# A second MLP computed in two phases through DRAM, its first product by a seven-product scheme

## The chip, the cores and the metric

One Trainium2 chip; the kernel runs on one of its cores. The metric is the device time of one execution in microseconds. Three executions of the kernel before took 925.81, 926.36 and 927.38 us, median 926.36.

## What is computed

Attention over 4 sequences of 576 tokens with 8 heads of 64, a window of 128 and a linear bias by distance; its output, 2304 tokens of 512, goes through two MLPs one after the other. The change is about the second.

```python
x = attention(q, k, v)                       # 2304 x 512
h = x @ w_in1                                # 2304 x 2048
g = where(h > 0, h, exp(min(h, 0)) - 1)
x = g @ w_out1                               # 2304 x 512
h = x @ w_in2                                # 2304 x 2048
g = maximum(0.01 * h, h)
return g @ w_out2                            # 2304 x 512
```

The weights arrive in float64. Everything is returned in float32.

## The kernel before

**Numbers.** Each float32 operand of an MLP product is split into a high part of type float32r (a cast on ACT) and a low part (a subtraction on DVE), and a product is the sum of three: high x high, high x low, low x high (split_mm). A weight in float64 is read as pairs of 32-bit words and turned into float32 by w_a1 and w_a2 on ACT and w_ts and w_add on DVE; w_hi and w_lo then split it.

**Tiles.** d_ff is cut into 16 pieces c of 128 (NC), d_model into 4 slices of 128 (NK), the tokens into blocks (BLK1 for the first MLP, BLK2 for the second), four of 512 and one of 256. For a block and a piece, the first product (mlp1_h, mlp2_h) has weights as the stationary operand and tokens as the moving one: 4 slices x 3 terms = 12 matmuls into one PSUM bank. ACT and DVE make g from it, split into high and low. The second product accumulates over the 16 pieces. In mlp1_y, w_out is stationary and tokens move; its output, still feature by token, is written to the DRAM tensor x2T. In mlp2_y, g's tokens are stationary (128 at a time) and 512 columns of w_out move; its banks hold rows of the output.

**Order.** All matmuls keep the order of the program (keep_in_program_order). Instructions on ACT, DVE, POOL and SP are ordered ahead of time by a planner with estimated durations, priority being the program's order; some runs of them (Ordered) are kept as written. Each engine then issues in that fixed order. Attention is interleaved with the first MLP's blocks. The last block of the first MLP (J = 4, lines 762 to 774) is interleaved with the second MLP's first block of 256 tokens, and layer 2's weights are converted there and later by w_tick. Then the second MLP runs block by block, mlp2_h one or two pieces ahead of mlp2_y (todo2, pend2).

**Buffers.** A tag names a ring of buffers. "w0" to "w15" hold one converted piece of weights each, or other things before and after; "eg", "gh" and "gl" hold g and its two parts, three buffers each; the eight PSUM banks are "y0" to "y3", "s0", "s1", "h" and "c".

Lines of the profile: L122 is the matmul in the helper matmul, and L113 the call in Ordered; so PE is read by tile names. h_ps is the first product of either MLP (layer 2's are written at line 699), y the second of layer 1, o_y, o_s and o_c the second of layer 2. L172 and L177 are w_a1 and w_a2, L533 to L537 the ELU and split in mlp1_h, L566 and L568 the evacuation of y, L684 to L688 the load and split of x2, L701 to L706 the leaky ReLU and split in mlp2_h.

Of the kernel before, what the change touches and what calls it, by code (L numbers as in the profile page):

```python
# [10 lines left out]
F32 = mybir.dt.float32  # L11
# [17 lines left out]
NB = NT // BLK  # L29

BLK1 = [(0, 512), (512, 256), (768, 512), (1280, 512), (1792, 512)]
BLK2 = [(0, 256), (256, 512), (768, 512), (1280, 512), (1792, 512)]


STAGING = [4 + c for c in range(12)] + [13, 14, 15, "pool"] + ["extra", "pool"] * 8
STAGED = (3, 2)
W1_EARLY = 12
LOADS = "ppppwppwppwwppwwwwwwww"

# [7 lines left out]
QK = 2 * BLK + P  # L47
FIRST_STARTS = [5, 9, 13, 15]
Y_LAG = 2
LAG2 = 4  # L50


def slope(h):
# [31 lines left out]
def attention_elu_leaky_kernel(  # L85
# [55 lines left out]


    W, raws, mids = {}, {}, {}
    pieces = [(layer, c) for layer in (1, 2) for c in range(NC)]
    at = {"load": 0, "a": 0, "b": 0, "c": 0}

    def w_load():
        k = at["load"]
        at["load"] += 1
        layer, c = pieces[k]  # L150
        w_in, w_out = ((w_in1, w_out1), (w_in2, w_out2))[layer - 1]

        kind = STAGING[k]
        if kind == "pool":
            raw = wrawp.tile([P, 2, DM, 2], I32, tag="wraw", name="wraw")
        elif kind == "extra":
            raw = extra.tile([P, 2, DM, 2], I32, tag="wraw2", name="wraw")
        else:
            raw = wp.tile([P, 2, DM, 2], I32, tag=f"w{kind}", name="wraw")
        for io, src in enumerate((w_in[c], w_out[c * P:(c + 1) * P, :])):  # L160
# [3 lines left out]
    def w_a1(k):  # L164
        high = raws[k][:, :, :, 1]
        f = wfp.tile([P, 2, DM], I32, tag="wf", name="wf")
# [57 lines left out]

    def w_tick(last):

        while at["load"] < min(last, max(at["c"] + STAGED[at["load"] >= NC], W1_EARLY)):
# [273 lines left out]
    def mlp1_h(J, cs, late_work=lambda: None):  # L501
# [3 lines left out]

        n = BLK1[J][1]
        xh, xl = X1[J]

        last = J == len(BLK1) - 1
# [28 lines left out]
        return hi, lo  # L538

    Y = {}  # L540
    xrp = None

    def mlp1_y(J, cs, gg):
        gh, gl = gg
# [9 lines left out]
                             start=cs[ci] == 0 and i == 0 and m % per == 0, stop=cs[ci] == NC - 1 and i == 2,  # L554
                             skip_group_check=True)
        if cs[-1] == NC - 1:
            if J == len(BLK1) - 1:

                all_ys = xrp.tile([P, NK, n], F32, tag="xr", name="xr")
            for i, y in enumerate(Y.pop(J)):  # L560
                if J == len(BLK1) - 1:
# [111 lines left out]
    attn.close()  # L673


    xrp = ctx.enter_context(tc.tile_pool(name="xr", bufs=1))
    gl2 = ctx.enter_context(tc.tile_pool(name="gl2", bufs=2))
    extra = ctx.enter_context(tc.tile_pool(name="wraw2", bufs=1))
    X2, O = {}, {}

    def x2_load(i):
        t0, n = BLK2[i]
        xr = xrp.tile([P, NK, n], F32, tag="xr", name="xr")
        nc.sync.dma_start(out=xr, in_=x2T[:, :, t0:t0 + n])  # L684
        x2 = x1p.tile([P, 2, NK, n], F32R, tag="x1", name="x2")
        for m in range(NK):
            nc.scalar.copy(x2[:, 0, m, :], xr[:, m, :])
            nc.vector.tensor_tensor(x2[:, 1, m, :], xr[:, m, :], x2[:, 0, m, :].bitcast(F32), op=ALU.subtract)  # L688
        X2[i] = x2[:, 0], x2[:, 1]

    def mlp2_h(i, c, k):
        n = BLK2[i][1]
        xh, xl = X2[i]
        ps = psp.tile([P, n], F32, tag="s0" if k < NC - LAG2 else ("h", "s0", "s1", "c")[k % (4 if i > 1 else 2)],
                      name="h2_ps")
        wih, wil = weights(2, c, 0)
        for kk in range(NK):
            s = slice(kk * P, (kk + 1) * P)
            split_mm(ps, wih[:, s], wil[:, s], xh[:, kk, :], xl[:, kk, :], kk == 0, kk == NK - 1)
        g = egp.tile([P, n], F32, tag="eg", name="g2")  # L700
        nc.scalar.activation(g, ps, AF.Prelu, alpha=0.01)  # L701
        pool = gl2 if k % 2 else glp
        hi = pool.tile([P, n], F32R, tag="gh", name="g2h")
        lo = pool.tile([P, n], F32R, tag="gl", name="g2l")
        nc.scalar.copy(hi, g)  # L705
        nc.vector.tensor_tensor(lo, g, hi.bitcast(F32), op=ALU.subtract)  # L706
        return hi, lo

    def mlp2_y(i, c, gg):
        t0, n = BLK2[i]  # L710
        hi, lo = gg
        woh, wol = weights(2, c, 1)
        if c == 0:
            O[i] = [psp.tile([P, DM], F32, tag=tg, name=f"o_{tg}")
                    for tg in (("y0", "y1", "y2", "y3") if i else ("s1", "c"))]
        for s in range(n // P):
            r = slice(s * P, (s + 1) * P)
            split_mm(O[i][s], hi[:, r], lo[:, r], woh, wol, c == 0, c == NC - 1)
            if c == NC - 1:
                rows = slice(t0 + s * P, t0 + (s + 1) * P)  # L720
                if i < len(BLK2) - 1:
                    os_ = egp.tile([P, DM], F32, tag="eg", name="os")
                else:

                    if s == 0:
                        O["os"] = xrp.tile([P, NK, DM], F32, tag="xr", name="xr")
                    os_ = O["os"][:, s]
                if i == len(BLK2) - 1 and s == n // P - 1:

# [12 lines left out]

    todo2 = [(0, c) for c in range(NC - LAG2)]
    for c in range(LAG2):
        todo2 += [(1, c), (0, NC - LAG2 + c)]
    todo2 += [(i, c) for i in range(1, len(BLK2)) for c in range(NC) if i > 1 or c >= LAG2]
    pend2, k = [], 0  # L750

    def mlp2():
        nonlocal k
        i, c = todo2[k]
        pend2.append((i, c, mlp2_h(i, c, k)))
        k += 1
        if i and c == 6 and i + 1 < len(BLK2):
            x2_load(i + 1)
        if len(pend2) > (1 if k <= NC - LAG2 else 2):
            mlp2_y(*pend2.pop(0))  # L760

    x2_load(0)
    J = len(BLK1) - 1
    for c in range(NC):
        g = mlp1_h(J, [c])
        mlp1_y(*pend.pop(0))
        pend.append((J, [c], g))
        while at["c"] < NC + c - Y_LAG:
            w_tick(2 * NC)
        if c >= LAG2:  # L770
            mlp2()
    x2_load(1)
    for x in pend:
        mlp1_y(*x)
# [57 lines left out]
```

## Time and profile before

| | us |
|---|---|
| median of three runs | 926.36 |
| the profiled execution | 926.94 |
| its span | 925.20 |
| PE busy | 914.6 |
| DVE busy | 407.1 |
| ACT busy | 403.8 |
| POOL busy | 118.0 |

PE is the matmul engine, DVE the vector engine, ACT the scalar engine, POOL the general one; SP only issues DMAs. The span is cut into stretches: the start and attention alone (to 63 us), attention with the first MLP (to 433 us), the first MLP's last block (433 to 566 us, with layer 2's first block beside it), the rest of the second MLP (to 919 us) and the tail. Busy times are sums over instructions; for PE they include waits that the pipeline hides, so its idle time is read from stretches and waits, and the price of one matmul in a stream from the chain of work, which counts only the time by which the end moves on.

### The profile page before, as it was taken

The page shows a single profiled execution, that of the slowest core. Times are in us where ns is not written, and L with a number is a line of the kernel's source. Part 1 is how long each engine was busy: PE and PEld are TensorE (multiplying, and loading weights), DVE is VectorE, ACT ScalarE, POOL GpSimd, SP SyncE. Part 2 cuts the span into 40 slices and gives each one's busy share as a digit, 9 for nine tenths or more (in the row PEclk, how much of TensorE's full clock was granted, in tenths as well). Part 3 has the DMA queues.
Part 4 walks back from the last instruction along what each step waited for, and adds up shares of the span by engine and source line. Part 5 has one row for each costly group of instructions (what it writes and reads, how often), then busy time and mean ns, then how long its engine had stood idle before and what let it go on. Part 6 is the DMA issues. An engine that isn't in the chain of part 4 may idle for free.

```text
span 925.2 us, 13025 instructions
## 1 busy us (share of the span) xinstructions
PE 914.6 (99%) x4885; PEld 747.9 (81%) x4885; DVE 407.1 (44%) x1034; ACT 403.8 (44%) x918; POOL 118.0 (13%) x281
## 2 busy tenths in 40 slices
PE   8999999999999999999999999999999999999998
PEld 5578878998887787888788888888888888888886
DVE  6798865655444454453566675211311131112111
ACT  7897854444344344333566665322322232222222
POOL 5702222323222211220000000000000000000000
PEclk9999999999999999999999999999999999999999
DMA  9842322222111021001244334100200010001001
GB/s 335 324 160 64 111 91 92 69 69 70 33 37 45 22 89 46 24 10 69 91 182 137 137 137 137 46 23 1 91 1 1 0 46 1 1 1 45 1 1 46
DMA packets 38495, 66.77 MB, mean 72 GB/s; under 512 B 3488, under 2 KB 22944, under 8 KB 38432
## 3 DMA queue, kind: packets, MB, share of 16 engines
q1 hardware_dynamic: 37712, 64.76, 20.4%
q10 hardware_dynamic: 720, 1.18, 0.3%
q8 instruction: 38, 0.62, 0.3%
q14 instruction: 25, 0.20, 0.1%
HBM read 56.49 MB, written 9.44 MB: 71 GB/s over the span
## 4 chain that ended last, share of the span: by engine, by line
PE 91%; DMA 6%; ACT 1%; DVE 1%; issue 0%; SPq 0%; ACTq 0%; DVEq 0%
PE h_ps L122 41%; PE y L122 20%; PE o_y L122 19%; PE s_ps L122 4%; PE av_ps L122 3%; DMA wraw<-in_w_out 3%; PE pt_ps L419 2%; DMA qkvr<-in_qkv 1%; PE o_s L122 1%; PE o_c L122 1%; DMA vr<-in_vp 1%; ACT wraw L177 0%; ACT wf L172 0%; DVE eg L535 0%; DMA x2T<-ys 0%
## 5 line engine op out<-in xcount | busy, mean ns | idle before, releaser
L122 PE MATMUL h_ps<-x,w 128*128 128x512 f32 (+1 forms) x1920 | 425.2, 370 | 1.7 <-DVE eg L535 0.7
L122 PEld LDWEIGHTS h_ps<-x,w 128*128 128x128 f32 x1920 | 335.4, 188 | 71.3 <-ACT x L113 4.0
L706 DVE TENSOR_TENSOR g2l<-g,g2h 128x512 fp32r<-128x512 f32 (+1 forms) x80 | 51.0, 637 | 272.3 <-ACT g2h L705 272.3
L122 PE MATMUL y<-gh,w 128*128 128x512 f32 (+1 forms) x640 | 157.7, 368 | 0.5 <-DVE ys L566 0.5
L122 PE MATMUL o_y<-w,g2h 128*128 128x512 f32 x512 | 157.7, 389 | 0.0
L701 ACT ACTIVATE g<-h_ps 128x512 f32<-128x512 f32 (+1 forms) x80 | 44.3, 554 | 255.3 <-PE h_ps L122 255.3
L122 PEld LDWEIGHTS y<-gh,w 128*128 128x128 f32 x640 | 113.8, 189 | 20.9 <-DVE ys L566 0.9
L122 PEld LDWEIGHTS o_y<-w,g2h 128*128 128x128 f32 x512 | 96.1, 188 | 20.0
L122 PE MATMUL o_y<-w,g2l 128*128 128x512 f32 x256 | 99.6, 389 | 0.0
L113 POOL TENSOR_SCALAR t<-t,stat 128x128 f32<-128x128 f32 (+3 forms) x160 | 71.5, 460 | 90.8 <-DVE stat L113 85.8
L113 ACT ACTIVATE t<-t,stat 128x128 f32<-128x128 f32 (+2 forms) x160 | 62.5, 393 | 42.6 <-DVE t L113 29.5
L533 ACT ACTIVATE eg<-h_ps 128x512 f32<-128x512 f32 (+1 forms) x80 | 44.0, 550 | 80.8 <-PE h_ps L122 78.6
L122 PE MATMUL y<-gl,w 128*128 128x512 f32 (+1 forms) x320 | 78.7, 368 | 0.0
L536 ACT CAST gh<-eg 128x512 fp32r<-128x512 f32 (+1 forms) x80 | 46.2, 577 | 73.9 <-DVE eg L535 67.0
L113 POOL TENSOR_SCALAR_AFFINE_SELECT pt<-pt 128x256 f32<-128x256 f32 (+1 forms) x112 | 45.2, 412 | 213.3 <-ACT pt L431 209.8
L537 DVE TENSOR_TENSOR gl<-eg,gh 128x512 fp32r<-128x512 f32 (+1 forms) x80 | 51.2, 640 | 38.3 <-ACT gh L536 38.1
L122 PEld LDWEIGHTS y<-gl,w 128*128 128x128 f32 x320 | 56.9, 189 | 10.0
L534 DVE TENSOR_SCALAR eg<-eg 128x512 f32<-128x512 f32 (+1 forms) x80 | 32.3, 405 | 63.1 <-ACT eg L533 61.2
L122 PEld LDWEIGHTS o_y<-w,g2l 128*128 128x128 f32 x256 | 48.1, 188 | 9.9
L113 DVE CUSTOM_DVE_ANT_0 t<-s_ps,bias 128x256 f32<-128x256 f32 (+4 forms) x160 | 51.6, 370 | 3.8 <-PE s_ps L122 3.2
L535 DVE TENSOR_TENSOR eg<-h_ps,eg 128x512 f32<-128x512 f32 (+1 forms) x80 | 50.9, 637 | 2.5
L705 ACT CAST g2h<-g 128x512 fp32r<-128x512 f32 (+1 forms) x80 | 46.2, 578 | 2.3
(60 smaller groups left out, 677.7 us busy)
## 6 DMA issues: line engine op xcount, KB each, us to landing
wraw<-in_w_in SPq DMA_DIRECT2D x32, 512.0 KB, 4.2
wraw<-in_w_out SPq DMA_DIRECT2D x32, 512.0 KB, 5.4
qkr<-in_kT SPq DMA_DIRECT2D x28, 192.0 KB, 2.8
xr<-x2T SPq DMA_DIRECT2D x4, 1024.0 KB, 5.3
qkr<-in_qT SPq DMA_DIRECT2D x28, 128.0 KB, 2.6
out<-os SPq DMA_DIRECT2D x14, 256.0 KB, 2.0
vr<-in_vp SPq DMA_DIRECT2D x16, 192.0 KB, 2.5
x2T<-ys SPq DMA_DIRECT2D x12, 256.0 KB, 2.6
```

The source lines that it names most:

```text
L113: ins = f(*args, **kw)
L122: tc.keep_in_program_order(nc.tensor.matmul(*args, **kw))
L419: tc.keep_in_program_order(nc.tensor.transpose(ps[:nk, col:col + n], t[:n, c:c + nk], ident[:n, :n]))
L533: nc.scalar.activation(g[:, :m], ps, AF.Exp)
L534: nc.vector.tensor_scalar(g[:, :m], g[:, :m], 1.0, -1.0, op0=ALU.min, op1=ALU.add)
L535: nc.vector.tensor_tensor(g[:, :m], ps, g[:, :m], op=ALU.max)
L536: nc.scalar.copy(hi[:, :m], g[:, :m])
L537: nc.vector.tensor_tensor(lo[:, :m], g[:, :m], hi[:, :m].bitcast(F32), op=ALU.subtract)
L701: nc.scalar.activation(g, ps, AF.Prelu, alpha=0.01)
L705: nc.scalar.copy(hi, g)
L706: nc.vector.tensor_tensor(lo, g, hi.bitcast(F32), op=ALU.subtract)
```

## The change

The second MLP is done in two phases. Phase one computes g for all tokens and writes it to a DRAM tensor g2T; phase two reads it back and does the second product.

In phase one, tokens are taken in 3 groups of 768 and d_ff in 8 pairs of pieces, 24 units. In a unit the first product is a 2 x 2 block product: two halves of the group (384 tokens), two halves of d_model (2 slices each), two pieces of d_ff. Strassen's scheme in Winograd's form makes the four blocks of the result from 7 block products. The sums of tokens (t1 to t4) are made by DVE (x2_job), the sums of weights by POOL (in_convert), the sums of results by DVE and by accumulating products in one bank. Products 1 and 2 share bank x, 6, 7 and 4 bank y, 5 and 3 bank z; two units' banks alternate. On PE the order is unit_a of a unit, unit_c of the unit before, unit_b.

Weights w_in2 are converted during the last block of layer 1, w_out2 in units 17 to 23 and in phase two's first block. That block of layer 1 has no matmuls of layer 2 beside it any more. In phase two, g2T is loaded four pieces at a time, split (g2_split), and used by mlp2_y as before. The block of 256 tokens is now the fourth of five.

The diff, cut:

```diff
+GRP = 768
+HALF = GRP // 2
+NP2 = NC // 2
+NU = NG * NP2
+OPERANDS = ("b11", "t2", "t1", "b21", "t3", "t4", "b22")
+OP_OF = {1: "b11", 2: "b21", 3: "b22", 4: "t4", 5: "t1", 6: "t2", 7: "t3"}
+W_OF = {1: 3, 2: 4, 3: 7, 4: 6, 5: 0, 6: 1, 7: 2}
...
-        tag = "s0" if last and cs[0] < LAG2 and (LAG2 - cs[0]) % 2 else "h"
-        if not last and cs[0] % 2 != (J == 0):
-            tag = "c"
+        tag = "c" if cs[0] % 2 != (J == 0) else "h"
...
-                if J == len(BLK1) - 1:
-                    ys = all_ys[:, i * per:i * per + per]
+                if i == 3:
+                    ys = glp.tile([P, per, n], F32, tag="gh", name="ys")
...
+    def in_convert(p):
+        k = ("in", p)
+        s = wp.tile([P, 8, 2 * P], F32, tag=f"w{p}", name="s")
+        w_ts(k)
...
+        dve.tensor_tensor(four.bitcast(I32), mids.pop(k), raw[:, :, :, 0], op=ALU.add)
+        for o, x, y, op in ((0, 5, 6, ALU.add), (1, 0, 3, ALU.subtract), (2, 3, 5, ALU.subtract), (7, 4, 1, ALU.subtract)):
+            pool.tensor_tensor(s[:, o], s[:, x], s[:, y], op=op)
...
+    def split_w(u, part):
+        s = S[u % NP2]
+        if part == 2:
+            t = wfp.tile([P, 2, 2, 2 * P], F32R, tag="wf", name="h2")
+            hi, lo = t[:, 0], t[:, 1]
+            cuts = [(0, 2, 6)]
+            H2[u] = hi, lo
+        else:
+            hi = wp.tile([P, 5, 2 * P], F32R, tag=f"w{8 + u % 2 * 2}", name="h1")
+            lo = wp.tile([P, 5, 2 * P], F32R, tag=f"w{9 + u % 2 * 2}", name="l1")
+            cuts = [(3, 5, 0), (0, 3, 0)]
+            H1[u] = hi, lo
+        for a, b, o in cuts:
+            nc.scalar.copy(hi[:, a:b], s[:, a + o:b + o])
+            nc.vector.tensor_tensor(lo[:, a:b], s[:, a + o:b + o], hi[:, a:b].bitcast(F32), op=ALU.subtract)
...
+    def x2_job(g, n):
...
+        def sub(o, x, y):
+            nc.vector.tensor_tensor(o, x, y, op=ALU.subtract)
+        def split(name, src):
...
+            nc.scalar.copy(t[:, 0], src)
+            nc.vector.tensor_tensor(t[:, 1], src, t[:, 0].bitcast(F32), op=ALU.subtract)
...
+        if n == 0:
+            split("b11", b(0, 0))
+            sub(b(0, 0), b(0, 1), b(0, 0))
+            sub(b(0, 1), b(1, 1), b(0, 1))
+        elif n == 1:
+            split("t1", b(0, 0))
+            sub(b(0, 0), b(1, 1), b(0, 0))
...
+    def product(m, u, bank, start):
...
+        for kk in range(2):
+            s = slice(kk * P, (kk + 1) * P)
+            split_mm(bank, wh[:, s], wl[:, s], xh[:, kk, :], xl[:, kk, :], start and kk == 0, kk == 1,
+                     skip_group_check=True)
...
+    def unit_a(u):
...
+        product(1, u, x, True)
+        s1 = small(glp, "gh", "s1")
+        nc.scalar.copy(s1, x)
+        product(6, u, y, True)
+        a = small(glp, "gl", "a")
+        nc.vector.tensor_tensor(a, y, s1, op=ALU.add)
+        product(5, u, z, True)
...
+    def unit_b(u):
+        product(2, u, x, False)
+        c11 = small(glp, "gh", "c11")
+        g2_out(u, 0, 0, c11, x)
+        product(7, u, y, False)
+        b = small(glp, "gl", "b")
+        nc.vector.tensor_tensor(b, y, s1, op=ALU.add)
+        c22 = small(egp, "eg", "c22")
+        nc.vector.tensor_tensor(c22, z, b, op=ALU.add)
+        g2_out(u, 1, 1, c22, c22)
...
+    def unit_c(u):
+        product(4, u, y, False)
+        c21 = small(egp, "eg", "c21")
+        nc.vector.tensor_tensor(c21, y, s1, op=ALU.add)
+        g2_out(u, 1, 0, c21, c21)
+        product(3, u, z, False)
+        c12 = small(egp, "eg", "c12")
+        nc.vector.tensor_tensor(c12, z, a, op=ALU.add)
+        g2_out(u, 0, 1, c12, c12)
...
+    late = {17: 0, 18: 1, 20: 2, 21: 3, 23: 4}
+    for u in range(NU):
+        g, p = divmod(u, NP2)
+        unit_a(u)
+        if u:
+            unit_c(u - 1)
+        unit_b(u)
+        if 0 < u < NU - 1:
+            split_w(u + 1, 1)
+        if u < NU - 1:
+            split_w(u + 1, 2)
+        if g and p == 0:
+            x2_job(g, 5)
+            x2_job(g, 6)
+        if g + 1 < NG:
+            if p == 2:
+                x2_load(g + 1)
+            elif 4 <= p <= 6:
+                x2_job(g + 1, p - 4)
+            elif p == 7:
+                x2_job(g + 1, 3)
+                x2_job(g + 1, 4)
...
+        if u in late:
+            out_work(late[u])
...
+    for n, (i, c) in enumerate(seq):
+        mlp2_y(i, c)
+        if n + 2 < len(seq):
+            g2_split(*seq[n + 2])
+        if c % 4 == 1:
+            g2_load(n // 4 + 4)
+        if i == 0 and c in (1, 3, 5):
+            out_work(5 + c // 2)
```

g2_out is a Prelu on ACT and a DMA of 128 x 384 to g2T from SP. out_work converts one pair of pieces of w_out2: w_a1, w_a2, w_ts, w_add, two casts and two subtractions of 512. In the last block of layer 1, piece c starts the conversion of pair c - 2 of w_in2 (w_first) and ends that of pair c - 3 (in_convert), which also loads pair c - 1; x2_load(0) stands at c = 9 and x2_job(0, ...) at c = 11 to 15.

## Rows read from the trace of the kernel before

**Rows 1.** The page's first part: busy us, share of the span, instructions of each engine.

```profile
PE 914.6 (99%) x4885; PEld 747.9 (81%) x4885; DVE 407.1 (44%) x1034; ACT 403.8 (44%) x918; POOL 118.0 (13%) x281
```

**Rows 2.** Stretches: busy us of PE, PEld, DVE, ACT, POOL; clock; DMA share; GB/s.

```profile
63.00:168.00 105.00, 104.54 (x640) 85.60 (x640) 78.69 (x208) 70.21 (x162) 27.02 (x54) 1.00 0.26 84
433.00:462.00 29.00, 28.34 (x127) 23.01 (x125) 14.88 (x25) 13.99 (x22) 0.00 (x0) 1.00 0.36 127
462.00:566.00 104.00, 103.32 (x527) 88.32 (x527) 70.47 (x108) 67.94 (x96) 0.00 (x0) 1.00 0.42 151
566.00:919.00 353.00, 353.00 (x1576) 292.99 (x1575) 61.49 (x93) 92.58 (x156) 0.00 (x0) 1.00 0.06 20
```

**Rows 3.** PE's waits from 433 to 925 us: in total, times, longest.

```profile
PE h_ps L122 <- DVE eg L535: 0.7, 1, 0.7
PE y L122 <- DVE ys L566: 0.5, 1, 0.5
PE h_ps L122 <- DVE w L113: 0.2, 1, 0.2
```

**Rows 4.** Chain of work in order of time: start us, us, what.

```profile
574.27 2.72 PE h_ps L122 x12
576.99 2.72 PE o_y L122 x12
579.71 1.43 PE h_ps L122 x12
581.14 0.69 PE o_s L122 x3
```

**Rows 5.** PE's groups by shape, 433 to 925 us: busy us, mean ns, idle before.

```profile
L122 PE MATMUL h_ps<-x,w 128*128 128x512 f32 x960 | 230.9, 389 | 0.7 <-DVE eg L535 0.7
...
L122 PE MATMUL h_ps<-x,w 128*128 128x256 f32 x192 | 25.8, 283 | 0.2 <-DVE w L113 0.2
```

**Rows 6.** ACT's groups by shape, whole span.

```profile
L705 ACT CAST g2h<-g 128x512 fp32r<-128x512 f32 x64 | 39.7, 621 | 1.9
...
L701 ACT ACTIVATE g<-h_ps 128x512 f32<-128x512 f32 x64 | 38.3, 598 | 245.1 <-PE h_ps L122 245.1
...
L172 ACT ACTIVATE wf<-wraw 128x1024 f32<-128x1024 f32 x32 | 36.7, 1146 | 0.9 <-ACT xr L568 0.5 <-DMA wraw<-in_w_out 0.4
L177 ACT ACTIVATE wraw<-wraw 128x1024 int32<-128x1024 uint32 x32 | 36.7, 1146 | 0.0
...
L705 ACT CAST g2h<-g 128x256 fp32r<-128x256 f32 x16 | 6.5, 406 | 0.4
...
L701 ACT ACTIVATE g<-h_ps 128x256 f32<-128x256 f32 x16 | 6.0, 376 | 10.2 <-PE h_ps L122 10.2
```

**Rows 7.** DVE's groups by shape, whole span.

```profile
L706 DVE TENSOR_TENSOR g2l<-g,g2h 128x512 fp32r<-128x512 f32 x64 | 44.2, 691 | 266.8 <-ACT g2h L705 266.8
...
L113 DVE CUSTOM_DVE_ANT_0 wraw<-wraw,wf 128x2048 uint16<-128x2048 uint16 x30 | 36.9, 1230 | 8.0 <-ACT wraw L177 6.6 <-DMA wraw<-in_w_in 0.6
...
L113 DVE TENSOR_SCALAR wf<-wf 128x1024 int32<-128x1024 int32 x32 | 22.4, 701 | 6.4 <-ACT wf L172 6.4
...
L706 DVE TENSOR_TENSOR g2l<-g,g2h 128x256 fp32r<-128x256 f32 x16 | 6.7, 419 | 5.5 <-ACT g2h L705 5.5
```

**Rows 8.** ACT in order of time, 652 to 655 us: start us, us, what.

```profile
652.03 0.60 ACT L701 ACTIVATE g<-h_ps 128x512 f32<-128x512 f32 x1 [4.19 <-PE h_ps L122]
652.52 0.61 ACT L687 CAST x<-xr 128x512 fp32r<-128x512 f32 x1
653.03 0.62 ACT L705 CAST g2h<-g 128x512 fp32r<-128x512 f32 x1
653.55 1.67 ACT L687 CAST x<-xr 128x512 fp32r<-128x512 f32 x3
```

**Rows 9.** DMA issues: KB each, median us to landing.

```profile
wraw<-in_w_in SPq DMA_DIRECT2D x32, 512.0 KB, 4.2
...
xr<-x2T SPq DMA_DIRECT2D x4, 1024.0 KB, 5.3
```

More of the change, by code (lines that the diff above doesn't have):

```diff
@@ L49 @@
 Y_LAG = 2
-LAG2 = 4
 def slope(h):
@@ L143, in attention_elu_leaky_kernel @@
     W, raws, mids = {}, {}, {}
-    pieces = [(layer, c) for layer in (1, 2) for c in range(NC)]
+    pieces = [(1, c) for c in range(NC)]
     at = {"load": 0, "a": 0, "b": 0, "c": 0}
@@ L225, in w_tick @@
     def w_tick(last):
-        while at["load"] < min(last, max(at["c"] + STAGED[at["load"] >= NC], W1_EARLY)):
+        while at["load"] < min(last, max(at["c"] + STAGED, W1_EARLY)):
             w_load()
@@ L673, in attention_elu_leaky_kernel @@
     attn.close()
[L676 to L689, printed above, removed]
@@ L691, in mlp2_h @@
-    def mlp2_h(i, c, k):
-        n = BLK2[i][1]
[L693 to L704, printed above, removed]
+    l2 = ctx.enter_context(tc.tile_pool(name="l2", bufs=1))
@@ new lines, in attention_elu_leaky_kernel, with raw_load @@
+    g2T = dram.tile([P, NC, NT], F32, name="g2T")
+    S, H1, H2, OP, Xr, W2, G, O = {}, {}, {}, {}, {}, {}, {}, {}
+    def raw_load(kind, i, home, tag):
+        raw = home.tile([P, 2, DM, 2], I32, tag=tag, name="wraw")
+        if kind == "in":
+            src = w_in2[2 * i:2 * i + 2].bitcast(I32).rearrange("c p (n w) -> p c n w", w=2)
+        else:
+            src = w_out2[2 * i * P:2 * (i + 1) * P, :].bitcast(I32).rearrange("(c p) (n w) -> p c n w", p=P, w=2)
+        for c in range(2):
+            nc.sync.dma_start(out=raw[:, c], in_=src[:, c])
+        raws[kind, i] = raw
@@ new lines, in attention_elu_leaky_kernel, with g2_out @@
+    ps2 = {}
+    def product(m, u, bank, start):
+        g = u // NP2
+        xh, xl = OP[g, OP_OF[m]]
+        i = W_OF[m]
+        wh, wl = (x[:, i - 6] for x in H2[u]) if i > 5 else (x[:, i] for x in H1[u])
+        for kk in range(2):
+            s = slice(kk * P, (kk + 1) * P)
+            split_mm(bank, wh[:, s], wl[:, s], xh[:, kk, :], xl[:, kk, :], start and kk == 0, kk == 1,
+                     skip_group_check=True)
+    def g2_out(u, c, half, tile_, src):
+        g, p = divmod(u, NP2)
+        nc.scalar.activation(tile_, src, AF.Prelu, alpha=0.01)
+        t0 = g * GRP + half * HALF
+        nc.sync.dma_start(out=g2T[:, 2 * p + c, t0:t0 + HALF], in_=tile_)
@@ new lines, in small @@
+    def small(home, tag, name):
+        return home.tile([P, HALF], F32, tag=tag, name=name)
+    def unit_a(u):
+        x, y, z = (psp.tile([P, HALF], F32, tag=tg[u % 2], name=nm)
+                   for tg, nm in ((("s0", "s1"), "px"), (("h", "c"), "py"), (("y0", "y1"), "pz")))
+        product(1, u, x, True)
[5 more added lines that the diff above has]
+        product(5, u, z, True)
+        ps2[u] = x, y, z, s1, a
@@ new lines, in attention_elu_leaky_kernel, with g2_load, g2_split @@
+    quads = [(i, c) for i in range(len(BLK2)) for c in range(0, NC, 4)]
+    def g2_load(n):
+        if n >= len(quads):
+            return
+        i, c = quads[n]
+        t0, w = BLK2[i]
+        g = (wp if n % 4 else l2).tile([P, 4, w], F32, tag=f"w{11 + n % 4}" if n % 4 else "xr", name="g2")
+        nc.sync.dma_start(out=g, in_=g2T[:, c:c + 4, t0:t0 + w])
+        for m in range(4):
+            G[i, c + m] = g[:, m]
+    def g2_split(i, c):
+        g = G[i, c]
+        n = BLK2[i][1]
+        hi = glp.tile([P, n], F32R, tag="gh", name="g2h")
+        lo = glp.tile([P, n], F32R, tag="gl", name="g2l")
@@ L741, in mlp2_y @@
                 nc.sync.dma_start(out=out[rows, :], in_=os_)
[L746 to L762, printed above, removed]
+    in_load(0)
+    in_load(1)
     J = len(BLK1) - 1
```

130 lines of the change are left out of this document (101 added, 29 removed).

## Prediction

> **What bounds the kernel now.** I read the engines' busy table first, then the stretches of the span, then TensorE's own waits, and last the chain of work in order of time.
>
> The busy table gives PE 914.6 us of a span of 925.2, and DVE and ACT 407.1 and 403.8 [rows 1]. The reader is to see that one engine has almost no free time and two have more than half of theirs.
>
> A busy matmul row can hide waits, so the stretches matter more. From 433 us, where the last block of the first MLP starts, PE is busy 28.34 of 29, 103.32 of 104 and then 353.00 of 353 us, always at a granted clock of 1.00, which is the 2.4 GHz level [rows 2]. What PE waits for from there to the end is three waits of 0.7, 0.5 and 0.2 us [rows 3]. The second MLP is bound by the number and length of its matmuls and by nothing else. Only a change that takes matmul time away can shorten it, and it must not make PE wait.
>
> The chain of work gives the price of a matmul in a stream, which the mean duration does not: matmuls overlap, so the mean of one is longer than its share of the stream. Twelve of 512 columns take 2.72 us, in the first product (h_ps) and in the second (o_y) alike, and twelve of 256 columns take 1.43 us [rows 4]. That is 226.7 ns and 119.2 ns each.
>
> **The change part by part. 1: fewer matmuls in the first product.** Before, layer 2 has 16 pieces of d_ff, 4 slices of the contraction and 3 terms of the high/low split, 192 matmuls for each token block. The four blocks of 512 tokens give 768 matmuls of 512 columns, the block of 256 gives 192 of 256. The rows count 960 and 192 [rows 5]; the 960 hold another 192 of layer 1's last block, which the change does not touch. Removed: 768 x 226.7 ns = 174.1 us and 192 x 119.2 ns = 22.9 us, together 197.0 us.
>
> After, there are 3 groups x 8 pairs = 24 units, each of 7 products, each of 2 slices x 3 terms: 24 x 7 x 6 = 1008 matmuls of 384 columns. No row shows this width. Between the two shown the price rises by (226.7 - 119.2) / 256 = 0.42 ns for a column, and 384 lies midway: 172.9 ns. Bounds: in proportion to the 512 row 170.0 ns, in proportion to the 256 row 178.8 ns. I take the line through both, since the two rows leave almost the same remainder over columns / 2.4 GHz (13.3 and 12.5 ns). Added: 1008 x 172.9 ns = 174.3 us (bounds 171.4 to 180.2). Result: 22.7 us less (bounds 25.6 to 16.8).
>
> **2: the second product.** Its matmuls have tokens as weights and always 512 columns: 18 token tiles x 16 pieces x 3 terms = 864, before and after. They cost the same 2.72 us for twelve. In the new phase two each piece needs one ACT cast (0.62 us) and one DVE subtraction (0.69 us) [rows 6, 7] for 2.72 us of PE, and g2T comes back in loads of 1 MB (5.3 us for the 1 MB load of x2T [rows 9]) for every four pieces, 10.9 us of PE. Both are covered; without that cover each load would cost its 5.3 us. The first four loads are issued during the last units and the tail after the last matmul is unchanged. Zero.
>
> **3: stalls that go.** The three waits of 0.7, 0.5 and 0.2 us [rows 3] belong to the conversion of layer 2's weights, to layer 2's matmuls inside the last block, and to the fourth evacuation of y, which waits for a DMA to free a buffer of "eg". The change takes the matmuls and that conversion out of the block and gives the evacuation a buffer of "gh". I count all as gone: 1.4 us less. If they stay, 0.
>
> **4: work added on ACT and DVE.** One unit is 42 matmuls, 7.26 us of PE. From the rows [rows 6, 7] by width (384 midway between 256 and 512; 768 by the same slope):
>
> DVE: five additions of 384 at 0.56 us and three subtractions for the weights (two of 512, one of 768: 0.69 + 0.69 + 0.96), together 5.1 us. ACT: the copy of P1 (0.51), four Prelus of 384 (0.49 each) and three casts (0.62 + 0.62 + 0.84), together 4.5 us. Both are below 7.26.
>
> In five units of a group (the loads of the next x2) DVE gets two operations of 768 more, 1.9 us, once three: 7.0 us, once 8.0. In units 17, 18, 20, 21 and 23 a piece of w_out is converted: DVE 0.70 + 1.23 + 2 x 0.69 = 3.3 us, so 8.4 in all; ACT 2 x 1.15 + 2 x 0.62 = 3.5 us, so 8.0 in all. These are over 7.26 by up to 1.2 us, but the units between them (19 and 22) have 2.1 us to spare, and back to back the three casts of one row take 1.67 us, 0.56 each instead of 0.62 [rows 8], so the sums are upper ends.
>
> What waits for it: PE needs product 1 copied before product 2 adds to the same bank, five products of 1.04 us after product 1's start, so 4.1 us after its end; c11's bank is needed again one unit later. The tightest is b: it is read from y after product 7, the last of a unit, and product 4 overwrites y three products later, 3.1 us. One addition of 0.56 us fits, behind a queue of at most about four such operations. I expect no wait in the steady state.
>
> **5: the preparation in the last block of layer 1.** It brings for each pair two passes on ACT (2.3 us) and two on DVE (1.9 us) and four subtractions on POOL, and later the first x2 jobs and weight splits. The block's own work per piece is an activation and a cast on ACT (1.2 us) and three operations on DVE (at most 2.1 us by the 512 row) for 5.44 us of PE; with the conversion 3.5 and 4.0. A POOL operation with two inputs has no row; POOL sits idle from 433 us, so up to 1.36 us each (5.44 / 4) is hidden, and results are wanted several pieces later. SP's queue takes eight pairs of loads of 512 KB at 4.2 us [rows 9]; what is queued behind them is the x2 load, needed at piece 11.
>
> **6: waits that remain.** Bounds: zero, and the excess of part 4 in full, 0.8 us twice and 1.2 us five times, 7.4 us (the x2 units at 7.0 have none). The nearest rows are two stretches in which DVE and ACT were as full as they will be: 63 to 168 us (DVE 75%, ACT 67%, PE idle 0.46 us of 105) and 462 to 566 us (68%, 65%, idle 0.68 us of 104) [rows 2]. That is 0.55 us in 100; the last block and the units take 87 + 174 us, so 1.5 us.
>
> **Sum.** The profiled execution took 926.94 us, 1.74 of it outside its span of 925.20. 926.94 - 22.7 - 1.4 + 1.5 = **904.4 us**. It lies 0.6 us above the median of 926.36 of the three runs shown, which is within their own spread of 1.6 us; no correction.
>
> **The rivals. A: the excess lands on PE.** ACT and DVE issue in a fixed order, so a long cast in front of an addition that PE waits for passes its delay on. Then part 6 takes its upper end, 7.4 instead of 1.5 us: 910. For it: the late units are full on both engines. Against it: 3 to 4 us of slack at every bank.
>
> **B: slower; each unit waits for its own weights.** In the code split_w for unit u+1 stands behind unit_b of u. If ACT and DVE ran in that order, the casts would sit behind the Prelu of c22, which comes after product 7, and product 1 of u+1 would wait: b 0.56, c22 0.56, Prelu 0.49, cast 0.62, subtraction 0.69 = 2.9 us, 23 times, 67 us: 971. It outweighs the gain of 22.5 us from 1.0 us for a unit on. Against it: the order is planned, not that of the code. An x cast of the next block stands in the trace between a Prelu and the g2h cast that directly follows it in the source [rows 8]. The inputs of split_w are ready a whole unit earlier and its buffers alternate, so a planner finds it a place.
>
> **C: the clock.** If the granted clock fell to its 1.2 GHz level in the units, a matmul there would cost at most twice, and even half of them would add 87 us: 990. All stretches stand at 1.00 [rows 2], through switches of the bank every three and every twelve matmuls [rows 4].
>
> The Trainium skill has a rule that speaks against this change: "TensorE: Matmul & The Clock Gate", section "A second HAM failure mode: psum-queue depth-cycling", says that cycling through PSUM banks between groups of matmuls can make the engine pause briefly and its clock swing between the two levels. By that rule the units, which change the bank after every six matmuls, would run partly at 1.2 GHz, as in C. The trace of before changes banks as often and shows no swing, so C gets 0.01.
>
> **How the numbers follow.** Forecast (901.5 to 908): 0.70. A (908 to 913): 0.15. Smaller gains up to 924: 0.02. B 0.10 and C 0.01. Within 0.2%: 0.02. The range leaves out B, C and the small gains: 901.5 (the low price of a matmul, 2.9 us less) to 912.5 (A, or the high price of a matmul, 5.9 us more, with two of A's). Faster by over 0.2% (about what a measurement of this kernel can tell from no change) 0.87, same 0.02, slower 0.11.
>
> **What would show it.** In the profile after: 1008 matmuls of 384 columns, six in 1.04 us in the chain; PE busy to within 1 or 2 us in all stretches from the last block on; DVE near 5.1 us of 7.26 in early units. It is wrong if PE waits between units for H1 (the weight splits), s1 or b, if six matmuls of 384 take over 1.07 us, or if the granted clock leaves 1.00.

## The result, and the profile after

| | before | after |
|---|---|---|
| median, us | 926.09 (925.60 to 927.38) | 910.60 (909.89 to 911.06) |
| the profiled execution | 926.94 | 911.06 |
| its span | 925.20 | 909.3 |

The change makes the kernel faster: the ratio is 0.983, with an interval of 0.9813 to 0.9847. Forecast were 904.4 us and a range of 901.5 to 912.5. The time is in the range, near its upper end. Between the profiled executions the gain is 15.9 us (926.94 - 911.06) where 22.5 were expected (926.94 - 904.4). The question of the experiments is where 6.7 us (911.06 - 904.4) went.

In the changed kernel the matmul helper is line 133 and Ordered line 124. px, py and pz are the three banks of a unit. L808 is the copy s1 and L822 is b; L824, L831 and L835 are c22, c21 and c12, all named c in the rows. L796 is the Prelu of g2_out and L798 its write to g2T. L179 and L184 are w_a1 and w_a2, L713 and L714 the casts and subtractions of a pair of w_out2, L732 the subtractions of split_w; L685 loads raw weights and L846 g2T. The busy table of after (columns as in [rows 1]):

```profile
PE 894.3 (98%) x4933; PEld 756.2 (83%) x4933; DVE 536.0 (59%) x1223; ACT 457.5 (50%) x1031; POOL 145.0 (16%) x313
```

Still one full engine, and two that have taken on 129 and 54 us. The stretches answer to [rows 2], with the columns of that group (PE, PEld, DVE, ACT, POOL busy, clock, DMA share, GB/s):

```profile
433.00:462.00 29.00, 29.00 (x130) 24.02 (x129) 15.44 (x22) 12.53 (x18) 5.80 (x8) 1.00 0.37 123
462.00:525.00 63.00, 63.00 (x280) 52.16 (x279) 51.03 (x63) 33.52 (x47) 21.23 (x25) 1.00 0.35 119
525.00:545.00 20.00, 19.36 (x111) 18.93 (x110) 13.53 (x21) 9.93 (x18) 0.00 (x0) 1.00 0.56 191
545.00:685.00 140.00, 139.93 (x808) 139.61 (x807) 112.61 (x181) 96.69 (x178) 0.00 (x0) 1.00 0.41 141
685.00:706.00 21.00, 16.94 (x91) 15.21 (x89) 13.62 (x25) 11.60 (x22) 0.00 (x0) 1.00 0.76 256
706.00:708.00 2.00, 1.44 (x8) 1.35 (x9) 1.10 (x3) 1.41 (x2) 0.00 (x0) 0.97 1.02 391
708.00:710.00 2.00, 2.00 (x6) 1.62 (x5) 1.84 (x3) 2.00 (x5) 0.00 (x0) 0.50 0.99 305
710.00:712.00 2.00, 2.00 (x7) 1.57 (x7) 1.89 (x4) 2.00 (x5) 0.00 (x0) 0.68 1.01 370
712.00:905.00 193.00, 193.00 (x853) 159.79 (x852) 64.63 (x99) 59.18 (x99) 0.00 (x0) 1.00 0.34 115
```

The last block of layer 1 (to 525 us), most units (to 685 us) and phase two (from 712 us) are full. PE has idle time at the second unit and in the last 21 us of phase one, and there the clock then falls to the 1.2 GHz level for some 3 us. TensorE's waits from 433 us to the end, as in [rows 3]:

```profile
PE pz L133 <- DVE c L824: 3.5, 2, 2.5
PE py L133 <- DVE b L822: 0.9, 2, 0.6
PE px L133 <- ACT s L808: 0.6, 1, 0.6
PE py L133 <- DVE c L831: 0.2, 1, 0.2
```

The chain of work shows the new price of a matmul, and the old one in phase two; it answers to [rows 4]:

```profile
544.36 1.04 PE px L133 x6
...
810.16 1.36 PE o_y L133 x6
811.52 0.68 PE o_s L133 x3
812.20 0.68 PE o_h L133 x3
```

**The account.** From the start of layer 1's last block (433.05 us before, 432.96 after) to the end of the last matmul (921.27 and 905.36) it takes 488.2 us before and 472.4 after: 15.8 us less. Six matmuls of 384 take 1.04 us, so 24 x 7 x 1.04 = 174.7 us were added where 197.0 were removed: 22.3 us. Before lost 2.9 us in that stretch beyond what its matmuls cost, which are gone too. 22.3 + 2.9 - 15.8 = 9.4 us that after loses. They can be placed by when units start: every unit takes 7.28 us but the second (8.20) and two of the last (7.65 and 7.74), and phase two starts 5.6 us late, together 7.4 us; the first nine matmuls of phase two take 3.65 instead of 2.04 us at the fallen clock, 1.6 us. That leaves 0.4 us without a place.

**Where the late stalls come from.** Four engines in order of time, after. TensorE first (start us, us, what, in brackets the idle time before it and what ended that):

```profile
698.65 1.31 PE L133 MATMUL pz<-x,h 128*128 128x384 f32 x6 [0.94 <-DVE c L824]
...
702.69 1.32 PE L133 MATMUL py<-x,h 128*128 128x384 f32 x6 [0.65 <-DVE b L822]
706.56 1.31 PE L133 MATMUL pz<-x,h 128*128 128x384 f32 x6 [2.55 <-DVE c L824]
```

DVE, which it waits for:

```profile
692.36 0.56 DVE L831 TENSOR_TENSOR c<-py,s 128x384 f32<-128x384 f32 x1 [2.07 <-DMA g2T<-c]
...
694.17 0.56 DVE L835 TENSOR_TENSOR c<-pz,a 128x384 f32<-128x384 f32 x1 [0.58 <-DMA g2T<-c]
...
696.84 1.29 DVE L714 TENSOR_TENSOR w<-wraw,w 128x512 fp32r<-128x512 f32 x2
698.05 0.55 DVE L824 TENSOR_TENSOR c<-pz,b 128x384 f32<-128x384 f32 x1
...
705.95 0.56 DVE L824 TENSOR_TENSOR c<-pz,b 128x384 f32<-128x384 f32 x1 [2.71 <-DMA g2T<-c]
```

ACT, which makes what is written to g2T:

```profile
688.92 0.53 ACT L796 ACTIVATE c<-c 128x384 f32<-128x384 f32 x1
691.73 1.14 ACT L179 ACTIVATE wf<-wraw 128x1024 f32<-128x1024 f32 x1 [2.28 <-DMA wraw<-in_w_out]
692.76 1.14 ACT L184 ACTIVATE wraw<-wraw 128x1024 int32<-128x1024 uint32 x1
693.80 0.51 ACT L796 ACTIVATE c<-c 128x384 f32<-128x384 f32 x1
```

SP, which issues the transfers:

```profile
685.80 0.81 SPq L685 DMA_DIRECT2D wraw<-in_w_out  x2
686.83 8.86 SPq L798 DMA_DIRECT2D g2T<-c  x7
695.77 0.41 SPq L846 DMA_DIRECT2D g<-g2T  x1
698.16 0.81 SPq L685 DMA_DIRECT2D wraw<-in_w_out  x2
699.23 2.77 SPq L798 DMA_DIRECT2D g2T<-c  x4
702.11 0.91 SPq L846 DMA_DIRECT2D g<-g2T  x1
```

Read from the last fence up. The raw half of w_out2 lies in one buffer (wraw), so the load of a pair is issued when the conversion before it has ended: 685.80, then 698.16, 12.4 us apart. From this late load two paths lead to PE. On the first, ACT's turn for w_a1 (L179) comes before the load has landed; ACT waits 2.28 us, and the rest of the conversion is late. On the second, the writes that were issued right behind the load land late. They hold the three buffers of "eg", DVE waits for a buffer (2.07 us before c21, 0.58 before c12), and PE for DVE. The chain of work (start us, us, what) goes by the second path, through a slow write behind each of three loads (of 661.53, 685.80 and 698.16 us):

```profile
663.39 6.46 DMA g2T<-c
...
687.76 6.32 DMA g2T<-c
...
694.64 1.22 DVE wraw L124
...
699.23 6.63 DMA g2T<-c
...
705.95 0.57 DVE c L824
```

The writes that DVE waits for at 692.36 and 694.17 were issued at 686.83 and 687.76, before ACT stood still (689.4 to 691.73). So they are not late because of ACT's wait, and the Prelu of c21 (693.80) could not have started before DVE had made c21, at 692.92. But the first path is close behind: w_add starts at 694.64 on DVE, and ACT's second pass, which it needs, ended only at 693.90. After that w_add and the subtractions of w_out2 (696.84) stand ahead of c22 (698.05), for which PE waits 0.94 us. At the end, 1 MB of w_out2 and 2 MB of g2T are loaded around the write of 699.23; its 6.63 us hold the buffer that the last c22 needs, and PE waits 2.55 us.

The issues of the whole span and of 690 to 708 us (KB each, median us to landing):

```profile
g2T<-c SPq DMA_DIRECT2D x96, 192.0 KB, 2.0
...
g2T<-c SPq DMA_DIRECT2D x8, 192.0 KB, 4.5
```

So the theory is: **the single raw buffer of w_out2 makes its loads and conversions late, by ACT's wait in its fixed order and by the writes behind the load, and a short ring of buffers carries that to PE.** The expectations below take the paths one at a time: what they call the theory of the single raw buffer is the first, and their DMA theory puts the second down to bursts of loads. Rivals: the busy time of ACT and DVE itself (rival A of the prediction), the loads for phase two, or the transfers as such. The early stall (8.20 us) is a DMA matter: ACT's copy s1 waits for a buffer of "gh" from which x2T is being written, while the next load of x2, 1.5 MB, goes ahead of the writes.

### The profile page after: what moved, and what is told of

Its sections match the earlier page's. It is cut to its first block, busy times and chain, and to the rows that moved or that the text cites. A ratio compares the mean times of both kernels' runs of the same rounds, so it can differ in the third digit from the quotient of the medians.

```text
span 909.3 us, 13924 instructions
## 1 busy us (share of the span) xinstructions
PE 894.3 (98%) x4933; PEld 756.2 (83%) x4933; DVE 536.0 (59%) x1223; ACT 457.5 (50%) x1031; POOL 145.0 (16%) x313
## 4 chain that ended last, share of the span: by engine, by line
PE 87%; DMA 3%; DVE 2%; ACT 1%; issue 1%; DVEq 0%; ACTq 0%
PE h_ps L133 21%; PE y L133 21%; PE o_y L133 12%; PE py L133 6%; PE o_s L133 5%; PE pz L133 4%; PE px L133 4%; PE s_ps L133 4%; PE o_h L133 4%; PE av_ps L133 3%; DMA g2T<-c 2%; PE pt_ps L426 2%; PE o_c L133 1%; DMA x2T<-ys 1%; DVE wraw L124 0%
## 5 line engine op out<-in xcount | busy, mean ns | idle before, releaser
L133 PE MATMUL h_ps<-x,w 128*128 128x512 f32 (+1 forms) x960 | 214.9, 373 | 0.9 <-ACT x L124 0.5
L133 PEld LDWEIGHTS h_ps<-x,w 128*128 128x128 f32 x960 | 166.1, 188 | 38.8 <-ACT x L124 4.0
L133 PE MATMUL o_y<-w,g2h 128*128 128x512 f32 x320 | 99.3, 392 | 0.0
L133 PE MATMUL py<-x,h 128*128 128x384 f32 x336 | 77.9, 335 | 1.1 <-DVE b L822 0.9
L539 DVE TENSOR_TENSOR gl<-eg,gh 128x512 fp32r<-128x512 f32 (+1 forms) x80 | 54.3, 678 | 37.4 <-ACT gh L538 37.3
L133 PEld LDWEIGHTS o_y<-w,g2h 128*128 128x128 f32 x320 | 60.4, 189 | 12.6
L133 PE MATMUL o_y<-w,g2l 128*128 128x512 f32 x160 | 62.7, 392 | 0.0
L133 PEld LDWEIGHTS py<-x,h 128*128 128x128 f32 x336 | 59.8, 188 | 2.1 <-DVE b L822 1.6
L133 PE MATMUL pz<-x,h 128*128 128x384 f32 x240 | 53.7, 336 | 3.6 <-DVE c L824 3.5
L796 ACT ACTIVATE c<-c 128x384 f32<-128x384 f32 x72 | 37.0, 523 | 36.3 <-DVE c L831 26.9
```

Of the source, the lines that this page charges most:

```text
L133: tc.keep_in_program_order(nc.tensor.matmul(*args, **kw))
L539: nc.vector.tensor_tensor(lo[:, :m], g[:, :m], hi[:, :m].bitcast(F32), op=ALU.subtract)
L796: nc.scalar.activation(tile_, src, AF.Prelu, alpha=0.01)
```

## The experiments

The runs were taken in groups, and the kernel before has a median from 926.1 to 927.7 us in them. So a difference of 1 to 2 us between medians of different groups tells nothing; each ratio is to the before of the same group.

**Is PE the bound? Product 1 is done twice in each unit**, so that a unit has eight products.

```diff
         product(1, u, x, True)
+        product(1, u, x, True)
```

> Product 1 is computed twice in every unit (same result), eight products for eight. PE is the bound in the units: 24 x 1.04 = 25.0 us more, less up to 3 us of waits that the longer units absorb: 932 to 936. If the units were bound by ACT and DVE: less than 12 us more, under 923.

Measured: 929.2 us (928.17 to 931.08), ratio 1.0022 (1.0013 to 1.0031) to before. 24 x 1.04 = 25.0 us of matmuls were added, and the time rose by 18.6 over after. That is less than was expected, but more than the 12 us of units bound by ACT and DVE. The other 6 us fit after's stalls: PE's waits from 520 us on are 0.7 and 0.4 us, at a clock of 1.00. Two things follow. With eight products the two phases would bring nothing over before, so leaving out one product of eight is the whole gain. And in units of 8.3 us the same buffers are enough: from 640 to 735 us ACT waits for raw weights only 0.9 us in all, and DVE for a write 1.5 us, once.

**Busy time alone: the weight splits of units 8 to 15 are repeated**, with no transfer added.

```diff
+        if 8 <= u <= 15:
+            split_again(u + 1, 2)
+            if 1 <= p <= 3:
+                split_again(u + 1, 1)
```

> In units 8 to 15 weight splits are done twice (same result): casts and subtractions of 512, in three units also of 512 and 768. Added per row prices, DVE would be busy 61.9 us of the 58.1 us of PE, as full as the late units or fuller, with no DMA added. Load theory: PE waits 4 us or more between 585 and 645 us, 914 or more. DMA theory: less than 1 us of waits there, 910 to 911.5.

Measured: 911.44 us (909.97 to 914.47), ratio 0.9836. The stretch of the heaviest units:

```profile
600.00:620.00 20.00, 20.00 (x117) 20.00 (x116) 20.00 (x34) 15.87 (x31) 0.00 (x0) 1.00 0.30 109
```

DVE is busy 20.00 of 20 us and PE, too. A full DVE, which the prediction's rival A was afraid of, costs PE nothing in these units, where nothing is converted: their slack at the banks is as large as part 4 said. The late waits stay: 4.0 us for c22 in the profiled execution (914.47 us, the longest of the four).

**The loads for phase two, issued behind the last unit's writes.**

```diff
+        if n in (1, 2, 3):
+            tc.keep_in_program_order(ins)
...
-    for n in (1, 2, 3):
-        g2_load(n)
...
     unit_c(NU - 1)
+    for n in (1, 2, 3):
+        g2_load(n)
```

> Only the SP queue changes: the three 1 MB loads of g2T (quads 1 to 3) are issued behind the last unit's writes. DMA theory (loads in a burst keep the units' writes from landing, the writes hold the buffers of eg and gh, DVE and PE wait for a buffer): o_y starts near 703 us instead of 707.7, the clock stays at 1.00, 904.5 to 907 us. Load theory (rival A: the conversions of w_out overload ACT and DVE in units 17 to 23): nothing changes, 909.5 to 911.5 us.

Measured: 911.88 us (910.5 to 915.82), ratio 0.9842 (0.9819 to 0.9866): no gain. In the profiled execution, the longest of the four, ACT still waits 2.17 us for wraw at 693.66, PE three times for c22 (2.4 us in all), and a wait of 1.8 us for the conversion of w_out has come up in phase two. These loads alone are not the cause.

**The second load of x2, issued behind unit 2's writes.**

```diff
-        nc.sync.dma_start(out=xr, in_=x2T[:, :, g * GRP:(g + 1) * GRP])
+        ins = nc.sync.dma_start(out=xr, in_=x2T[:, :, g * GRP:(g + 1) * GRP])
+        if g == 1:
+            tc.keep_in_program_order(ins)
```

> The second group's x2 load (1.5 MB) is issued behind unit 2's writes instead of ahead of the last block's x2T writes at 524.9 us. DMA theory: the x2T writes land in 3 to 5 us instead of 8.4 to 9.6, unit 1 takes 7.28 us instead of 8.20, 0.9 us less in all (909.7), and the late stalls stay. Load theory: no change (910.6), since no conversion runs there.

Measured: 910.44 us (908.73 to 912.0), ratio 0.982 (0.9805 to 0.9834). From 525 to 540 us PE is busy 15.00 of 15, so the 0.9 us of the second unit are gone; the profiled execution shows them lost again in the last units (waits of 4.1, 0.7 and 0.5 us, clock 0.66 from 700 to 710 us).

**Transfers alone: two idle loads of 1 MB behind that x2 load**, in units 2 and 3, where nothing is converted.

```diff
+                for home, tag in ((wp, "w15"), (wrawp, "wraw")) if g == 0 else ():
+                    t = home.tile([P, 4, 512], F32, tag=tag, name="idle_load")
+                    tc.keep_in_program_order(nc.sync.dma_start(out=t, in_=x2T[:, :, :512]))
```

> Built on the kernel with the late x2 load: two more loads of 1 MB that nothing reads are issued right behind it, in units 2 and 3, where ACT and DVE have only a unit's own work and nothing is converted. 3.5 MB at some 390 GB/s is 9 us. DMA theory: the units' g2T writes in that stretch land in 5 to 9 us instead of 2.0, PE waits there and the kernel is 1 to 4 us slower than the one with the late load alone. Load theory: no wait there, within 0.5 us of it.

Measured: 914.63 us (914.24 to 915.84), 4.2 more than the kernel it was made from. The stretches around the idle loads:

```profile
550.00:560.00 10.00, 10.00 (x60) 10.00 (x59) 8.46 (x12) 6.94 (x12) 0.00 (x0) 1.00 1.02 376
560.00:570.00 10.00, 8.06 (x37) 7.74 (x36) 8.26 (x14) 5.02 (x11) 0.00 (x0) 0.83 0.76 254
```

With the DMA engines full (1.02) PE stands 1.94 us later on and the clock falls to 0.83. Late writes can stall PE without any conversion, behind a burst of 3.5 MB (the x2 load of 1.5 MB and the two idle ones). The last units of after load 3 MB between 695.77 and 702.11 us, so this shows that such a stall is possible there, not its share.

**The conversion moved: its loads pinned at later units** (18, 20, 21 and 23), the conversions at units 17, 19, 21, 22 and 23; and **the same with 64 of the 512 columns converted**, the rest of w_out2 set to zero.

```diff
-    late = {17: 0, 18: 1, 20: 2, 21: 3, 23: 4}
+    late = {17: 0, 19: 1, 21: 2, 22: 3, 23: 4}
...
+        if u in (18, 20, 21):
+            out_load({18: 1, 20: 2, 21: 3}[u])
```

> Reference for the next kernel: the loads of w_out are pinned at fixed places of the SP queue (units 18, 20, 21, 23), conversion complete. Both theories: 908 to 913 us, waits again at the end of the units.

> Same SP queue as the kernel with pinned loads, all bytes still loaded, but only 64 of 512 columns of w_out are converted and the rest is zero, so the output is not the reference's. ACT loses about 3 us and DVE about 3 us in each of the late units. DMA theory: within 1.5 us of the pinned kernel, the same waits for DMA g2T<-c. Load theory: the late waits vanish, 5 to 7 us less than the pinned kernel.

Measured: 917.79 us (917.11 to 919.32) in full and 905.74 (904.18 to 906.85) with 64 columns. In the full one PE waits 3.6 us for b and 4.2 us in phase two for weights that are not yet converted. b (704.31) stands on DVE behind a c12 that waits 2.68 us for a write, and behind w_add (703.17), which waits for ACT's two passes over a raw half; ACT had waited 1.56 us for that half, until 700.99. So here ACT's wait is on the way to PE. The light one loads the same bytes and has waits of 1.2, 0.7, 0.6 and 0.2 us. So 12 us hang on the conversion. This alone could speak for its arithmetic; after the run with a full DVE it rather speaks for the round of load, wait and convert through a single buffer.

**The first matmuls of phase two ahead of the last unit's products 4 and 3.**

```diff
     g2_split(*seq[0])
+    mlp2_y(*seq[0])
     unit_c(NU - 1)
```

> mlp2_y of the first block's first piece (12 matmuls, 2.72 us) stands before unit_c of the last unit on PE; DMAs and conversions stay. Both theories: the 0.65 and 2.55 us of idle time are filled with work and the clock stays at 1.00, so 1.6 us at the lower clock go too: 4 us less, 906 to 907.5. If the idle time and not the clock were all that cost, 3 us less (907.5); if the wait only moves, 910.

Measured: 912.7 us (911.03 to 913.88), ratio 0.9844. A miss: PE's waits for c22 shrink to 1.0 us, and 1.8 and 1.6 us of waits for the split of g2 take their place.

**Two raw buffers: odd pairs of w_out2 are loaded into a buffer that is free by then**, so that each load is issued one conversion earlier. The arithmetic and its places in the program stay; the planner, which works from them, orders ACT and DVE anew.

```diff
-        raw_load("out", q, wrawp, "wraw")
+        raw_load("out", q, *((x1p, "x1") if q % 2 else (wrawp, "wraw")))
...
-        if q + 1 < NP2:
-            out_load(q + 1)
+        if q + 2 < NP2:
+            out_load(q + 2)
...
             out_load(0)
+            out_load(1)
```

> w_out's raw halves alternate between their own buffer and the then free buffer of layer 1's inputs, so each load is issued one conversion earlier; all arithmetic stays. Theory of the single raw buffer (ACT's in-order conversion waits for a load that could not be issued earlier, the activations behind it are late): ACT's waits on the raw weights go, the PE waits between 690 and 704 us go or halve, what is left is the wait at the end of the last unit behind a late write and the clock after it: 906 to 908.5 us. Rival (the arithmetic of the conversion itself, or the loads for phase two, set the stalls): 910 to 911.5, with the same waits as the changed kernel.

Measured: 906.57 us (905.94 to 908.53), ratio 0.9781 (0.9766 to 0.9796). Between 655 and 712 us ACT no longer waits for raw weights, and of PE's waits these are left:

```profile
PE py L133 <- DVE l L732: 1.4, 1, 1.4
PE px L133 <- ACT s L808: 0.9, 1, 0.9
PE py L133 <- DVE b L822: 0.7, 1, 0.7
```

No wait for c22, and the clock is 1.00 throughout. So the late stalls hang on the buffer and not on the amount of arithmetic, which is the same. By which of the two paths isn't shown by this run: ACT's wait is gone, but the conversions also end earlier and stand elsewhere in DVE's order. The writes have not become quick; between 640 and 712 us DVE still waits 4.3 us for them (6.6 in after), only no longer in front of c22. What is left: a weight split of DVE behind a c12 that waits for its buffer, the x2 load of the second unit, and b in the last unit, where no products of a next unit stand between product 7 and product 4.

**Which of the two effects of the earlier loads counts? An idle load of 1 MB is put back** into this kernel, ahead of the write of c22 in the last unit but one, where after has its load of w_out2.

```diff
+        if u == NU - 2:
+            t = wp.tile([P, 4, 512], F32, tag="w6", name="idle_load")
+            for c in range(2):
+                tc.keep_in_program_order(nc.sync.dma_start(out=t[:, 2 * c:2 * c + 2], in_=x2T[:, 2 * c:2 * c + 2, :512]))
         g2_out(u, 1, 1, c22, c22)
```

> The kernel with two raw buffers, and besides 1 MB is loaded into a free buffer in the last unit but one, just ahead of the write of its c22, where the changed kernel has its load of w_out; nothing reads it. It puts the load back that competes with the writes and leaves ACT free of the wait. If the transfer's competition with the writes makes the last stall: the wait behind c22 comes back, 908.5 to 910 us. If ACT's wait for the raw weights makes all of it: as with two raw buffers, 906 to 907.5.

Measured: 907.6 us (903.97 to 908.84), ratio 0.9788 (0.9761 to 0.9815), between the two expectations. In the profiled execution PE's wait for c22 comes back with 1.5 us of after's 3.5, by the second path: DVE waits 1.62 us for a write ahead of it. The span is 905.9 instead of 904.2 us, but the intervals of the ratios overlap. So this one load's competition with the writes is worth 0.6 us by the ratios and 1.7 by the spans, of some 4, which is within what these runs can tell from nothing. It does not follow that ACT's wait has the rest. The earlier loads of w_out2 compete with writes in both kernels, and no run takes ACT's wait away alone; how the 4 us are shared between the two paths stays open.

**Is the ring of three the link? Single raw buffer again, and c22 of the last units in two buffers of its own.**

```diff
-        c22 = small(egp, "eg", "c22")
+        c22 = small(x1p, "x1", "c22") if u > 16 else small(egp, "eg", "c22")
```

> The changed kernel, its single raw buffer kept, with c22 of the last seven units in two buffers of its own instead of the ring of three that c21, c12 and c22 share. ACT's waits and the transfers stay. Theory (three buffers, held until late writes have landed, carry the delay to DVE and PE): DVE's long waits for g2T's writes go, PE's waits for c22 go, 905.5 to 908 us. If late Prelus reach PE in another way, or the buffers are not the link: 910 to 911.5.

Measured: 914.49 us (912.76 to 915.52), ratio 0.9869: slower than after, where a gain was expected. PE's waits in it:

```profile
PE o_y L133 <- ACT w L713: 3.3, 1, 3.3
PE o_y L133 <- ACT g2h L855: 2.1, 1, 2.1
PE py L133 <- DVE b L822: 0.7, 1, 0.7
PE pz L133 <- DVE c L824: 0.6, 1, 0.6
```

The link was seen rightly: the waits for c22 fall from 3.5 to 0.6 us, and phase two begins at 702.39 instead of 707.71 us. But the ring alone gains nothing: the loop of load and conversion goes on as slowly as before, and now it meets PE in phase two. ACT there, and the matmul that waits for it:

```profile
742.46 1.12 ACT L179 ACTIVATE wf<-wraw 128x1024 f32<-128x1024 f32 x1 [4.12 <-DMA wraw<-in_w_out]
...
746.61 0.50 PE L133 MATMUL o_y<-w,g2h 128*128 128x512 f32 x1 [3.26 <-ACT w L713]
```

That after has no such wait is probably because its stalls in phase one had given the conversions the time that they lack here; this was not tried by itself, and the wait of 2.1 us for g2h has no explanation here. The ring of "eg" is where the delay reached PE, the raw buffer is what makes it.

**The best version: two raw buffers, the loads of phase two behind the last writes, the second x2 load behind unit 2's.** It joins three of the edits above; the main lines:

```diff
+        raw_load("out", q, *((x1p, "x1") if q % 2 else (wrawp, "wraw")))
...
+        if g == 1:
+            tc.keep_in_program_order(ins)
...
     unit_c(NU - 1)
+    for n in (1, 2, 3):
+        g2_load(n)
```

> As the run with two raw buffers, and besides the loads of phase two stand behind the last unit's writes and the second input load behind unit 2's. Theory of the single raw buffer: with the conversion's loads early and the queue free of bursts only some 1 to 2 us of PE waits are left, no fall of the clock: 902.5 to 904.5 us. Rival (the conversion's arithmetic sets the stalls): 909 to 911.

Measured: 904.9 us (903.58 to 906.93), ratio 0.9763 (0.9748 to 0.9778); the profiled execution took 903.58, its span 901.9. The stretches that answer to after's 525 to 545 and 545 to 685 us:

```profile
525.00:545.00 20.00, 20.00 (x117) 20.00 (x116) 11.17 (x20) 10.33 (x21) 0.00 (x0) 1.00 0.36 131
545.00:685.00 140.00, 140.00 (x810) 140.00 (x809) 117.58 (x189) 98.45 (x180) 0.00 (x0) 1.00 0.47 160
```

Two waits are left, 0.8 and 0.7 us. The median is 0.4 us over the expected range. It beats both kernels, and its advantage of 1.7 us over the run with two raw buffers lies within the two intervals.

## Why the prediction was right, and where it was short

The time lies in the range, but in part by luck. The upper end stands where it does because of A's excess of busy time and of a dear matmul, and neither made the time what it is. Against the sum, part 1 was short by 0.4 us and part 3 gave 1.5 us more; part 6 took 7.9 us more than was put down. (The sum itself comes to 904.3, not 904.4.)

**What bounds: right.** Eight products instead of seven cost 18.6 us for 25.0 us of matmuls; only the stalls lay in between.

**Part 1: right.** 173.3 ns for a matmul of 384 columns instead of 172.9, and 22.3 us of gain instead of 22.7. The line through the two widths held.

**Part 2: right.** Phase two runs at 2.72 us for twelve without a wait once its clock is back, beside its casts and loads. The cover is not endless: with c22 apart it lacked weights, for 3.26 us in one place.

**Part 3: short by half.** The removed stalls were counted at the three waits' 1.4 us; by the account, before lost 2.9 us in that stretch. Part of the difference may be that a wait costs more than its idle time: the second unit of after came 0.92 us late for a wait of 0.64.

**Part 4: right on the work.** The weight split of 768 columns takes DVE 0.95 us and b 0.55 us, as interpolated (0.96 and 0.56):

```profile
L732 DVE TENSOR_TENSOR l<-s,h 128x768 fp32r<-128x768 f32 x21 | 20.0, 950 | 0.0
...
L822 DVE TENSOR_TENSOR b<-py,s 128x384 f32<-128x384 f32 x21 | 11.6, 554 | 6.3 <-PE py L133 6.3
```

Its sentence on b left one unit out. In the last, product 4 follows product 7 directly, without three products of slack, and PE waits there for about 0.65 us in every run that keeps the order.

**Part 5: right.** From 433 to 525 us PE does not wait once. A POOL operation with two inputs takes 0.87 us, under the 1.36 that could be hidden.

**Part 6: the step that failed.** 1.5 us of remaining waits were taken, from stretches as full as the new ones; it was 9.4. The fault is in how it was sized, not in the number alone: the bounds (0 to 7.4) were made of busy time on ACT and DVE, and in the run that added busy time alone it cost nothing. What cost was not on its list: the load of a pair through a single buffer, about 12 us a round, the instruction in a fixed order that waits for it (w_a1), the writes behind that load (6.3 to 6.6 us on the chain instead of 2.0), and the three buffers that these writes hold. The prediction counted conversions in five of the last seven units, but priced them as work that can be done at any time, not as a round of load, wait and convert. The clock's 1.6 us had no term at all. By its own signs the step was wrong, too: PE waited for s1 (0.6 us) and for b (0.9 us), and the clock left 1.00.

**The rivals.** A gave 910, and the time is 910.6; yet the excess of busy time did not land on PE where it was tried alone. Something of A is left in one place, where subtractions of w_out2 stand ahead of c22 (696.84). The agreement of the times is a coincidence of sizes. B did not occur: no unit waited for H1. Of C a trace remained: the clock fell once, after a wait, and cost 1.6 us.

**The skill's rule.** The Trainium skill ("TensorE: Matmul & The Clock Gate", section "A second HAM failure mode: psum-queue depth-cycling") reports a swinging clock where a kernel cycles through banks and the engine pauses briefly between groups of matmuls. The units change bank after every six matmuls, and their clock is 1.00 from 545 to 685 us, with PE busy 139.93 of 140 us, so the trace shows neither the pauses nor the swing there; the clock fell only after PE had stood still.

## What to carry to other kernels

When work is moved into a loop, don't only add its busy time. Follow each load to the instruction that waits for it, and ask what stands behind that instruction on its engine; and ask which writes stand behind the load, and which buffers they hold until they land. A conversion with a single raw buffer is a round of load and work whose length sets a pace of its own; a second buffer gave back some 4 of the 6.7 us that were missing. If another edit only removes the place where such a round reaches the busy engine, the wait comes out elsewhere. And when the trace is read for a cause, see whether the wait that catches the eye is on the chain of work: here ACT's longest wait for raw weights was not.

## What was not expected of the hardware

- The clock fell for a short wait. After 2.55 us of PE idle, with 0.94 and 0.65 us shortly before, the granted clock was 0.97 from 706 to 708 us and then 0.50 (the 1.2 GHz level) and 0.68 in the next two stretches of 2 us, and that cost 1.6 us. Around the wait of 1.94 us in the run with idle loads it was 0.83 (560 to 570 us). Waits of 1.40, 0.93 and 0.65 us in the run with two raw buffers left it at 1.00.
- A write of 192 KB to DRAM takes 2.0 us to land in the median of the span, and 4.5 between 690 and 708 us, among loads that fill the DMA engines at the end of it (share 1.02, 391 GB/s from 706 to 708 us); three in the chain took 6.3 to 6.6. The writes here hold buffers, so the loads that compete with them matter even where nobody waits for those loads.
